# One decode layer, four edits: head 0's softmax on its own, head 6's scores by halves, c and x in SyncE's queue, block-diagonal queries by GpSimd

## The chip, the cores and the metric

The kernel runs on one core of a Trainium2 chip. TensorE (PE) multiplies matrices into PSUM, which has eight banks of 512 float32 per partition; VectorE (DVE), ScalarE (ACT) and GpSimd (POOL) work on tiles of 128 partitions; SyncE (SP) only issues transfers here, and sixteen DMA engines carry them. Each engine runs its instructions in the order in which they were written and waits on semaphores for the others. The metric is device time in microseconds (us), the median of the runs. Times inside an execution count from the first instruction of its profile, its span.

## The reference, cut to what matters

One token (D = 512) goes through attention over a cache of 32768 positions, 32 query heads on 8 key and value heads of 128, and then through a dense layer with ReLU. Both are modulated by a condition vector c.

```python
mod = (_silu(c) @ w_mod).reshape(c.shape[0], 6, 1, -1)
sa, ca, ga, sb, cb, gb = (mod[:, 0].copy(), mod[:, 1].copy(), ...)
h = _layernorm(x, axis=-1) * (1 + ca) + sa
# _A_ref(h): q = h @ wq, 32 heads of 128; each cache head serves 4 of them
scores = jnp.einsum('bhqd,bhkd->bhqk', q, k) * Dh ** (-0.5)
p = _softmax(scores, axis=-1)
o = jnp.einsum('bhqk,bhkd->bhqd', p, v)          # then @ wo
x = x + ga * _A_ref(h, A_k_cache, A_v_cache, A_wq, A_wo)
h = _layernorm(x, axis=-1) * (1 + cb) + sb
x = x + gb * _B_ref(h, B_w1, B_w2)               # relu(h @ w1) @ w2
```

Keys and values are 8 tiles of 8.39 MB each, bfloat16. With the weights that makes 149.4 MB, and every byte is read once.

## The kernel before, in words

**The ring and the stream of loads.** SBUF holds a ring of three slots of 8.39 MB. What is loaded into them, in order, is: w_mod and w_q together (`first`), K0, K1, V0, K2, K3, V1, K4, K5, V2, K6, K7, V3, V4, V5, V6, V7, and then W_o, w1 and w2 (`load_tail`). Each `Tenant` takes the slot of the tenant three before it, so `Tenant.load` (line 228) makes its transfer wait for the last use of that one: K3 waits for the scores of head 1, which read K1, V1 for the product PV(0) with V0, K4 for the scores of head 2, V4 for those of head 6, V5 for those of head 7. In full: slot 0 holds `first`, V0, V1, V2, V3, V6; slot 1 holds K0, K2, K4, K6, V4, V7; slot 2 holds K1, K3, K5, K7, V5 and the tail. All these transfers are issued by SyncE, one after the other; one that waits holds up those behind it. c and x, 1 KB each, are brought into `cx_row` (16 rows of 64) by two transfers from GpSimd's queue (line 285), and the transfers of K0 and K1 wait for both.

**The prologue.** VectorE spreads `cx_row` into a block-diagonal tile (line 327), PE turns it into columns, and the sigmoid, the modulation (24 matmuls with w_mod), a layer norm and the query projection (32 matmuls with w_q) follow. `qrep_sb` (line 456) then holds all queries, repeated per strip of 32 partitions.

**Keys.** A key tile arrives with positions on the partitions. VectorE turns it in place, four transposes (`turn`, line 469) of 128x4096 float32 words, a quarter each. Then `scores` runs 64 matmuls of 512 columns: the weights are `qbd`, where the four queries of the head stand block-diagonally (one block of 32 partitions per strip), shifted from step to step so that all results gather in two banks, one per half G of the tile. A first half needs turns 0 and 1, a second half turns 2 and 3. `build_qbd(g)` (line 463) writes the queries of head g into `qbd` with four ScalarE copies; it waits for the scores of head g - 1, which read the same tile. Only head 7 runs its scores by halves; all others run both halves in one loop after their four turns.

**Softmax.** Heads go in pairs. `maxima` (line 500) reduces a head's two banks; `softmax` turns the maxima on PE (line 510), reduces and spreads them on VectorE (lines 511 and 513), turns them back (line 517), and ScalarE makes the bias and one exponential per head (line 521) into `Pall`. `turn_p` (line 530) transposes both heads' P at once; `sums` and `inverse` (line 544) make the reciprocal of the sum. PV(g) multiplies P of head g with value tile g (64 matmuls). `blocks(g)` (lines 573 and 576) and `o_cols(g)` gather its result in Y and in columns.

**Order.** It is written out by hand. `k_event(h)` gives: the sums of the last pair, four turns, the scores, the queries of the next head, the inverse, and the blocks of an open product; after an odd head, the maximum of the even one before it. `v_event(g)` follows after heads 1, 3 and 5 with g = 0, 1, 2: the odd head's maximum, the softmax of the pair, `turn_p`, and PV(g). So PV(0) stands behind the scores of head 1, PV(1) behind those of head 3, and PV(2) behind those of head 5. After head 7 come PV(3), the last softmax, PV(4) to PV(7) and the output projection, the second layer norm and the dense layer. `keep_clock` inserts idle matmuls there.

Of the kernel before, what the change touches and what calls it, by code (L numbers as in the profile page):

```python
# [9 lines left out]
ALU = mybir.AluOpType  # L10
AX = mybir.AxisListType
# [10 lines left out]
class Flow:  # L22
# [12 lines left out]
    def op(self, eng, run, r=(), w=(), after=(), n=1, dma=False):  # L35
        o = Op(eng, run, n, dma)
        deps = list(after)
        for k in r:
            deps += self.writers.get(k, [])
        for k in w:  # L40
            deps += self.writers.get(k, [])
            deps += self.readers.get(k, [])
        known = self.known[eng]
        for d in deps:
            if d.eng == eng and eng == "pe" and not d.dma:
                continue
            if known.get(d.src, 0) >= d.idx:
                continue
            o.waits.append(d)
        best = {}  # L50
        for d in o.waits:
            if d.src not in best or best[d.src].idx < d.idx:
                best[d.src] = d
        o.waits = []
        for d in sorted(best.values(), key=lambda d: -len(d.clock)):
            if known.get(d.src, 0) >= d.idx:
                continue
            o.waits.append(d)
# [12 lines left out]
        self.ops.append(o)  # L71
        return o
# [5 lines left out]
    def semaphores(self):  # L78
        sems = {e: self.tc.alloc_semaphore(f"of_{e}") for e in self.engine if e != "sp"}
        at = {e: 0 for e in sems}  # L80
        for o in self.ops:
            if o.dma:
                o.sem, o.val = self.tc.alloc_semaphore(f"of_{o.src[0]}{o.src[1]}"), 16
            elif o.used:
                at[o.eng] += o.n
                o.sem, o.val = sems[o.eng], at[o.eng]
# [15 lines left out]
def kernel(  # L102
    ctx, tc, A_x, A_k_cache, A_v_cache, A_wq, A_wo, B_x, B_w1, B_w2, c, w_mod, out,
):
    nc = tc.nc
    P = 128
# [62 lines left out]
    QW = P + 4 * 7  # L169
    qbd = sb("qbd", [P, 4, QW], BF16)  # L170
    mask4 = sb("mask4", [P, REP])
    cmask, rsel_f, rsel = {}, {}, {}
    for n in sorted({n * REP for _, n in WOP}):
        cmask[n] = sb(f"cmask{n}", [P, P // n])
        rsel_f[n] = sb(f"rsel_f{n}", [P, n])
        rsel[n] = sb(f"rsel{n}", [P, n], BF16)
    smask = sb("smask", [16, 4])
    place32 = sb("place32", [P, 32])
# [52 lines left out]
    def rows(src):  # L231
        return src.rearrange("p a b -> p (a b)") if len(src.shape) == 3 else src

    first = Tenant()
    first.load("wm", 0, KT * 6 * D, rows(w_mod.rearrange("(p kt) n -> p kt n", p=P)))
    WQ0 = KT * 6 * D
    first.load("wq", WQ0, KT * Hq * Dh, rows(A_wq.rearrange("(p kt) n -> p kt n", p=P)))
    TMP0 = WQ0 + KT * Hq * Dh
# [41 lines left out]

    wo, w1, w2, spare = [], [], [], []

    for i, src in enumerate((c[0], A_x[0, 0])):
        op(
            "pool", lambda i=i, src=src: nc.gpsimd.dma_start(
                out=cx_row[8 * i:8 * i + 8], in_=src.rearrange("(a n) -> a n", a=8)),
            (), [("cx", i)], dma=True,
        )

    for kind, g in order[:2]:  # L290
        load_tile(kind, g, after=f.writers[("cx", 0)] + f.writers[("cx", 1)])

    def identity(t, key):
        pool(lambda: G_.memset(t, 0.0), (), [key])
# [12 lines left out]
    col_at = col.rearrange("p (kt w) -> p kt w", w=CW)[:, :, 96]  # L307
    first.use(pool(lambda: G_.memset(col, 0.0), (), ["col"]))

    dve(lambda: V.memset(bank(0), 0.0), (), ["b0"])  # L310
    dve(lambda: V.memset(bank(1), 0.0), (), ["b1"])
    dve(lambda: V.memset(bank(2), 0.0), (), ["b2"])
    dve(lambda: V.memset(bank(3), 0.0), (), ["b3"])
    dve(lambda: V.memset(bank(6)[:, 0:REP + KT], 0.0), (), ["b6"])
    oT_ps, attnT_ps = bank(6)[:, 0:REP], bank(6)[:, REP:REP + KT]
    small = bank(7)
# [2 lines left out]
        out=pick8, in0=ident_bf[0:16, 0:8], in1=ident_bf[0:16, 8:16], op=ALU.add), ["ident_bf"], ["pick8"])  # L319

    def fold(o, src, how, key, **kw):
        dve(lambda: V.tensor_reduce(out=o, in_=src.rearrange(how, **kw), op=ALU.add, axis=AX.X), ["ident_f"], [key])

    fold(cmask[8], ident_f, "p (c r) -> p c r", ("cmask", 8), r=8)
    dve(lambda: V.tensor_copy(out=cx_sel, in_=cmask[8][0:16, 0:2]), [("cmask", 8)], ["cx_sel"])
    cx_bd = tmpB.bitcast(BF16)[0:16, 0:512].rearrange("p (b n) -> p b n", b=8)
    first.use(dve(lambda: V.tensor_tensor(  # L327
        out=cx_bd, in0=cx_row.unsqueeze(1).to_broadcast([16, 8, D // 8]),
        in1=pick8.unsqueeze(2).to_broadcast([16, 8, D // 8]), op=ALU.mult,
    ), [("cx", 0), ("cx", 1), "pick8"], ["tmpB"]))  # L330

    def xc_mm(inc):
        for kt in range(KT):
# [11 lines left out]

    fold(mask4, ident_f, "p (x q) -> p q x", "mask4", q=REP)
    for n in cmask:
        if n != 8:
            fold(cmask[n], ident_f, "p (c r) -> p c r", ("cmask", n), r=n)
        fold(rsel_f[n], ident_f, "p (c r) -> p r c", ("rsel_f", n), r=n)  # L350
        dve(lambda n=n: V.tensor_copy(out=rsel[n], in_=rsel_f[n]), [("rsel_f", n)], [("rsel", n)])
    fold(smask, ident_f[0:16, 0:16], "p (s q) -> p s q", "smask", q=REP)
    fold(place32, ident_f, "p (j m) -> p m j", "place32", m=32)
    fold(rowpick, ident_f, "p (j m) -> p j m", "rowpick", m=32)
    qsel = mask4[0:16, :]

# [99 lines left out]
    dve(lambda: V.tensor_copy(out=qrep_sb, in_=qrep_ps), ["b5"], ["qrep"])  # L456

    def build_qbd(g):
        d, s = qbd, qrep_sb
        for a in range(4):  # L460
            o = AP(d.tensor, d.offset + 32 * a * d.ap[0][0] + 4 * 7 + 32 * a, [[d.ap[0][0], 32], [QW, 4], [1, 4]])
            i = AP(s.tensor, s.offset + 32 * a * s.ap[0][0] + REP * g, [[s.ap[0][0], 32], [Hq, 4], [1, 4]])
            act(lambda o=o, i=i: S.copy(out=o, in_=i), ["qrep"], ["qbd"])  # L463


    def turn(h, q):
        t = K[h]
        x = t.ap[:, CH * Dh * q:CH * Dh * (q + 1)].bitcast(F32)
        t.use(dve(lambda: V.transpose(out=x, in_=x), [("k", h, q)], [("kt", h, q)]))  # L469
# [56 lines left out]
    def turn_p(hs):  # L526
        n, i, k = len(hs), hs[0] % 2, hs[0] % 4
        keys = [("P", h % 4) for h in hs]
        pf = Pall[:, k:k + n, :].rearrange("p h f -> p (h f)")
        dve(lambda: V.transpose(out=pf, in_=pf), keys, keys)  # L530
# [277 lines left out]
    f.semaphores()  # L808
    with tc.tile_critical():
        f.emit()  # L810
        nc.scalar.wait_ge(sent.sem, 16)

# [28 lines left out]
```

## Time and profile before

The kernel took 365.78 us, median of 3 runs (364.48 to 366.78). The profiled execution took 364.59 us, its span is 362.8 us.

| | busy us | share of the span | instructions |
|---|---|---|---|
| PE matmuls | 281.1 | 77% | 1283 |
| PE weight loads | 115.2 | 32% | 1283 |
| VectorE | 195.5 | 54% | 187 |
| ScalarE | 31.5 | 9% | 69 |
| GpSimd | 4.2 | 1% | 17 |
| SyncE's DMA queue | | 96% of 16 engines | 4760 packets, 149.43 MB |

The mean rate is 412 GB/s over the span, and TensorE's mean granted clock 0.924. Where times to landing are given, they count from the issue of a transfer to the moment when its waiters may go on. In stretches of a microsecond the DMA share scatters and can come out above 1; that it is 0 means that nothing moved. "L160" is the line of the matmul helper, so matmuls are told apart by what they read: `ring,qbd` are scores, `ring,Pall` are products with V.

### The profile page before, as it was taken

What the parts mean: (1) busy time and instruction counts of PE and PEld (TensorE: products, weight loads), DVE (VectorE), ACT (ScalarE), POOL (GpSimd) and SP (SyncE); (2) the same over time, 40 slices, a digit from 0 to 9 for tenths busy, and PEclk for the clock granted to TensorE, in tenths of its full rate; (3) what the DMA queues carried; (4) which work ended last, traced back from release to release, by engine and by line L of the source; (5) the groups of instructions that cost most, each with busy time, mean ns of one, the idle gap of its engine ahead of it and who ended that gap; (6) DMA issues with size and microseconds to landing.
All of it is one profiled execution on the core that took longest, in us unless ns stands there. A gap on an engine that the chain in (4) does not pass through costs nothing.

```text
span 362.8 us, 4525 instructions
## 1 busy us (share of the span) xinstructions
PE 281.1 (77%) x1283; PEld 115.2 (32%) x1283; DVE 195.5 (54%) x187; ACT 31.5 (9%) x69; POOL 4.2 (1%) x17
## 2 busy tenths in 40 slices
PE   0659005969199978889496979598999999799996
PEld 0223002424034423323142423133343334334434
DVE  4430797960399992169998039999220500321142
ACT  1020300000700000040000050000000400000000
POOL 4000000000000000000000000000000000000000
PEclk9987655999869998999699999989999999999999
DMA  8998999899988989998999899989998999999970
GB/s 317 431 502 369 462 455 441 376 462 462 426 383 347 457 369 448 455 462 369 448 455 449 376 455 455 441 376 462 455 434 385 455 405 448 419 425 430 414 302 2
DMA packets 4831, 149.52 MB, mean 412 GB/s; under 512 B 600, under 2 KB 856, under 8 KB 1752
## 3 DMA queue, kind: packets, MB, share of 16 engines
q1 hardware_dynamic: 4760, 149.43, 96.0%
q8 instruction: 4, 0.07, 0.1%
q14 instruction: 3, 0.02, 0.0%
q0 software_dynamic: 64, 0.00, 0.0%
HBM read 149.42 MB, written 0.00 MB: 412 GB/s over the span
## 4 chain that ended last, share of the span: by engine, by line
PE 49%; DVE 24%; DMA 23%; ACT 2%; issue 1%; POOL 0%; SPq 0%; POOLq 0%
PE banks L160 48%; DMA ring<-in_A_k_cache_dram 21%; DVE ring L469 19%; DMA cx_row<-in_A_x_dram 2%; DVE Pall L530 1%; ACT Pall L521 1%; DVE Y L576 1%; DVE m_p L500 1%; ACT L521 0%; DVE Y L573 0%; DVE Mrow L511 0%; ACT qbd L463 0%; PE banks L510 0%; DVE ring L619 0%; PE banks L517 0%
## 5 line engine op out<-in xcount | busy, mean ns | idle before, releaser
L160 PE MATMUL banks<-ring,qbd 128*128 x512 | 122.4, 395 | 40.8 <-DVE ring L469 29.9
L469 DVE STREAM_TRANSPOSE ring<-ring 128x4096 f32<-128x4096 f32 x32 | 139.3, 4410 | 4.3 <-DMA ring<-in_A_k_cache_dram 4.3
L160 PE MATMUL banks<-ring,Pall 128*16 x512 | 120.7, 386 | 10.1 <-DVE Lexp L531 6.5
L160 PEld LDWEIGHTS banks<-ring,qbd 128*128 x512 | 50.6, 99 | 109.8 <-issue 59.8
L160 PEld LDWEIGHTS banks<-ring,Pall 128*16 x512 | 45.2, 89 | 81.7 <-issue 38.1
L500 DVE TENSOR_REDUCE m_p<-banks 128x1 f32<-128x1024 f32 x8 | 9.6, 1203 | 53.1 <-PE banks L160 53.1
L463 ACT COPY qbd<-qrep_sb 32x16 bf16<-32x16 bf16 x32 | 6.4, 201 | 187.8 <-PE banks L160 186.3
L160 PE MATMUL banks<-ring 128*128 x56 | 17.1, 480 | 3.9 <-DVE ring L437 2.4
L530 DVE STREAM_TRANSPOSE Pall<-Pall 128x2048 bf16<-128x2048 bf16 x4 | 9.2, 2312 | 10.0 <-ACT Pall L521 10.0
L590 DVE TENSOR_TENSOR oT_sb<-banks,Linv 128x4 bf16<-128x4 f32 x8 | 1.2, 153 | 20.7 <-PE banks L160 20.7
L160 PEld LDWEIGHTS banks<-ring 128*128 x56 | 6.6, 118 | 13.5 <-issue 9.7
L600 DVE CAST o<-banks 128x4 bf16<-128x4 f32 (+2 forms) x4 | 0.7, 166 | 18.0 <-PE banks L160 18.0
L160 PE MATMUL banks<-cx_sel,ring 16*128 16x2 bf16 x4 | 0.3, 171 | 11.2 <-DVE ring L327 11.2
L521 ACT ACTIVATE Pall<-banks,nbias 128x1024 bf16<-128x1024 f32 x8 | 8.8, 1109 | 0.1
L576 DVE SCALAR_TENSOR_TENSOR Y<-banks,smask,Y 16x128 f32<-16x128 f32 x24 | 8.1, 339 | 0.8
L511 DVE TENSOR_REDUCE Mrow<-banks 2x4 f32<-2x128 f32 x4 | 1.1, 279 | 13.8 <-PE banks L510 13.8
L573 DVE TENSOR_SCALAR Y<-banks,smask 16x128 f32<-16x128 f32 x8 | 2.5, 314 | 9.9 <-PE banks L160 9.9
L476 ACT COPY banks<-zero_t 128x2048 f32<-128x2048 f32 x4 | 7.5, 1868 | 0.1
L421 ACT ACTIVATE std_ln<-negvar_ln,eps_t 128x1 f32<-128x1 f32 x2 | 0.6, 295 | 64.8 <-DVE negvar_ln L418 64.8
L444 DVE STREAM_TRANSPOSE ring<-banks 128x512 f32<-128x512 f32 x2 | 1.3, 695 | 8.9 <-PE banks L160 8.9
L160 PE MATMUL banks<-qbd,ident_bf 128*128 128x512 bf16 x19 | 5.6, 381 | 0.0
L160 PE MATMUL banks<-mask,Y 16*128 16x4 f32 x16 | 3.0, 258 | 1.8 <-DVE Y L576 1.8
(112 smaller groups left out, 69.1 us busy)
## 6 DMA issues: line engine op xcount, KB each, us to landing
ring<-in_A_v_cache_dram SPq DMA_DIRECT2D x3, 4096.0 KB, 25.6
ring<-in_A_wq_dram SPq DMA_DIRECT2D x1, 4096.0 KB, 19.6
ring<-in_A_v_cache_dram SPq DMA_DIRECT2D x2, 2048.0 KB, 32.4
ring<-in_w_mod_dram SPq DMA_DIRECT2D x1, 3072.0 KB, 10.4
ring<-in_A_wo_dram SPq DMA_DIRECT2D x1, 2048.0 KB, 25.8
ring<-in_B_w_dram SPq DMA_DIRECT2D x1, 1344.0 KB, 32.3
ring<-in_A_wo_dram SPq DMA_DIRECT2D x1, 1024.0 KB, 27.9
ring<-in_A_wo_dram SPq DMA_DIRECT2D x2, 512.0 KB, 29.1
```

The lines of the kernel that those rows point to most:

```text
L160: return T.matmul(o, lhsT=lhsT, rhs=rhs, start=start, stop=stop, skip_group_check=True)
L444: first.use(dve(lambda i=i: V.transpose(out=q_cols[:, i, :], in_=bank(2 + i)), [f"b{2 + i}"], ["tmpB" if i == 0 else "col"]))
L463: act(lambda o=o, i=i: S.copy(out=o, in_=i), ["qrep"], ["qbd"])
L469: t.use(dve(lambda: V.transpose(out=x, in_=x), [("k", h, q)], [("kt", h, q)]))
L476: act(lambda: S.copy(out=banks[:, b:b + n, :].rearrange("p g f -> p (g f)"), in_=zero_t.to_broadcast([P, 512 * n]),), ["zero"], [f"b{b + i ...
L500: dve(lambda: V.reduce_max(out=m_p[:, i:i + 1], in_=banks[:, b:b + 2, :].rearrange("p g f -> p (g f)"), axis=AX.X), [f"b{b}", f"b{b + 1}"] ...
L511: dve(lambda: V.tensor_reduce(out=Mrow[0:n], in_=small[0:n, 0:P].rearrange("o (x q) -> o q x", q=4), op=ALU.max, axis=AX.X), ["b7"], ["Mrow"])
L521: act(lambda h=h, b=b, j=j: S.activation(out=Pall[:, h % 4, :], in_=banks[:, b:b + 2, :].rearrange("p g f -> p (g f)"), func=ACT.Exp, bias ...
L530: dve(lambda: V.transpose(out=pf, in_=pf), keys, keys)
L573: dve(lambda: V.tensor_scalar(out=Y, in0=o[:, 0], scalar1=smask[:, 3:4], scalar2=None, op0=ALU.mult), [f"b{b}", "smask"], ["Y"])
L576: dve(lambda s=s: V.scalar_tensor_tensor(out=Y, in0=o[:, s], scalar=smask[:, 3 - s:4 - s], in1=Y, op0=ALU.mult, op1=ALU.add), [f"b{b}", "Y ...
L590: dve(lambda: V.tensor_tensor(out=o_g, in0=oT_ps, in1=Linv[:, g % 4, :], op=ALU.mult), ["b6", ("Linv", g % 4)], [("oT", g)])
```

## The change

Four edits and some smaller ones.

- c and x are loaded by five transfers in SyncE's queue, behind w_mod and ahead of w_q: c as 8 rows of 64, x as 4, 2, 1 and 1 rows. K0 and K1 no longer wait for them.
- Head 0's maximum and softmax are written between the third and fourth turn of K1, its `turn_p` after the fourth, both ahead of the scores of head 1. After those, only head 1's softmax and `turn_p` are left ahead of PV(0).
- Head 6's scores run by halves, as head 7's do: the first after turns 0 and 1, four matmuls a loop step, the second after turns 2 and 3, eight a step.
- `build_qbd` becomes one GpSimd product of the queries with a 0/1 tile `strip`, 64 elements per partition, over all 128 partitions.
- The smaller ones: one memset for four banks, the 0/1 tiles reduced straight to bfloat16 by a maximum instead of a sum and a copy, one tile (`strip`) more, and transfers that share semaphores where one is known to be over before the next is issued.

```diff
     def semaphores(self):
+        lanes = []
         for o in self.ops:
             if o.dma:
-                o.sem, o.val = self.tc.alloc_semaphore(f"of_{o.src[0]}{o.src[1]}"), 16
+                free = [x for x in lanes if o.clock.get(x[1].src, 0) >= x[1].idx]
...
+                free[0][2] += 16
+                o.sem, o.val = free[0][0], free[0][2]
...
     first.load("wm", 0, KT * 6 * D, rows(w_mod.rearrange("(p kt) n -> p kt n", p=P)))
+    cx_of = [(c[0], 0, 8), (A_x[0, 0], 8, 4), (A_x[0, 0], 12, 2), (A_x[0, 0], 14, 1), (A_x[0, 0], 15, 1)]
+    for i, (src, r, n) in enumerate(cx_of):
+        at = 64 * (r % 8)
+        op(
+            "sp", lambda src=src, r=r, n=n, at=at: nc.sync.dma_start(
+                out=cx_row[r:r + n], in_=src[at:at + 64 * n].rearrange("(a n) -> a n", a=n)),
+            (), [("cx", i)], dma=True,
+        )
...
-    for i, src in enumerate((c[0], A_x[0, 0])):
-        op(
-            "pool", lambda i=i, src=src: nc.gpsimd.dma_start(
-                out=cx_row[8 * i:8 * i + 8], in_=src.rearrange("(a n) -> a n", a=8)),
-            (), [("cx", i)], dma=True,
-        )
-
     for kind, g in order[:2]:
-        load_tile(kind, g, after=f.writers[("cx", 0)] + f.writers[("cx", 1)])
+        load_tile(kind, g)
...
-    dve(lambda: V.memset(bank(0), 0.0), (), ["b0"])
...
+    dve(lambda: V.memset(banks[:, 0:4, :], 0.0), (), [f"b{i}" for i in range(4)])
...
-    fold(cmask[8], ident_f, "p (c r) -> p c r", ("cmask", 8), r=8)
-    dve(lambda: V.tensor_copy(out=cx_sel, in_=cmask[8][0:16, 0:2]), [("cmask", 8)], ["cx_sel"])
+    fold(cx_sel, ident_f[0:16, 0:16], "p (c r) -> p c r", "cx_sel", r=8)
...
+    fold(strip, ident_f, "p (a c) -> p a c", "strip", a=4)
...
     def build_qbd(g):
-        d, s = qbd, qrep_sb
-        for a in range(4):
...
-            act(lambda o=o, i=i: S.copy(out=o, in_=i), ["qrep"], ["qbd"])
+        o = AP(qbd.tensor, qbd.offset + 4 * 7, [[qbd.ap[0][0], P], [QW, 4], [32, 4], [1, 4]])
+        pool(lambda: G_.tensor_tensor(
+            out=o, in0=qrep_sb[:, :, REP * g:REP * (g + 1)].unsqueeze(2).to_broadcast([P, 4, 4, REP]),
+            in1=strip.unsqueeze(1).unsqueeze(3).to_broadcast([P, 4, 4, REP]), op=ALU.mult,
+        ), ["qrep", "strip"], ["qbd"])
...
         for u in range(4):
+            if h == 1 and u == 3:
+                maxima(0)
+                softmax((0,))
             turn(h, u)
-            if h == LAST and u % 2:
+            if h >= LAST - 1 and u % 2:
                 scores(h, (u // 2,), 1 + u // 2)
-        if h < LAST:
+        if h == 1:
+            turn_p((0,))
+        if h < LAST - 1:
             scores(h, (0, 1), 1)
...
-        if h % 2:
+        if h % 2 and h > 1:
             maxima(h - 1)
...
         maxima(hs[-1])
-        softmax(hs)
+        now = hs if g else hs[1:]
+        softmax(now)
         finish()
-        turn_p(hs)
+        turn_p(now)
```

More of the change, by code (lines that the diff above doesn't have):

```diff
@@ L80, in semaphores @@
         at = {e: 0 for e in sems}
+        lanes = []
         for o in self.ops:
             if o.dma:
-                o.sem, o.val = self.tc.alloc_semaphore(f"of_{o.src[0]}{o.src[1]}"), 16
+                free = [x for x in lanes if o.clock.get(x[1].src, 0) >= x[1].idx]
+                if not free:
+                    lanes.append([self.tc.alloc_semaphore(f"of_dma{len(lanes)}"), None, 0])
+                    free = lanes[-1:]
+                free[0][1] = o
+                free[0][2] += 16
+                o.sem, o.val = free[0][0], free[0][2]
             elif o.used:
@@ L171 @@
     mask4 = sb("mask4", [P, REP])
-    cmask, rsel_f, rsel = {}, {}, {}
+    cmask, rsel = {}, {}
     for n in sorted({n * REP for _, n in WOP}):
         cmask[n] = sb(f"cmask{n}", [P, P // n])
-        rsel_f[n] = sb(f"rsel_f{n}", [P, n])
         rsel[n] = sb(f"rsel{n}", [P, n], BF16)
     smask = sb("smask", [16, 4])
-    place32 = sb("place32", [P, 32])
+    place32, strip = sb("place32", [P, 32]), sb("strip", [P, 4])
     rowpick = sb("rowpick", [P, KT])
@@ L308 @@
     first.use(pool(lambda: G_.memset(col, 0.0), (), ["col"]))
-    dve(lambda: V.memset(bank(0), 0.0), (), ["b0"])
-    dve(lambda: V.memset(bank(1), 0.0), (), ["b1"])
-    dve(lambda: V.memset(bank(2), 0.0), (), ["b2"])
-    dve(lambda: V.memset(bank(3), 0.0), (), ["b3"])
+    dve(lambda: V.memset(banks[:, 0:4, :], 0.0), (), [f"b{i}" for i in range(4)])
     dve(lambda: V.memset(bank(6)[:, 0:REP + KT], 0.0), (), ["b6"])
@@ L321, in fold @@
     def fold(o, src, how, key, **kw):
-        dve(lambda: V.tensor_reduce(out=o, in_=src.rearrange(how, **kw), op=ALU.add, axis=AX.X), ["ident_f"], [key])
-    fold(cmask[8], ident_f, "p (c r) -> p c r", ("cmask", 8), r=8)
-    dve(lambda: V.tensor_copy(out=cx_sel, in_=cmask[8][0:16, 0:2]), [("cmask", 8)], ["cx_sel"])
+        dve(lambda: V.tensor_reduce(out=o, in_=src.rearrange(how, **kw), op=ALU.max, axis=AX.X), ["ident_f"], [key])
+    fold(cx_sel, ident_f[0:16, 0:16], "p (c r) -> p c r", "cx_sel", r=8)
     cx_bd = tmpB.bitcast(BF16)[0:16, 0:512].rearrange("p (b n) -> p b n", b=8)
@@ L329 @@
         in1=pick8.unsqueeze(2).to_broadcast([16, 8, D // 8]), op=ALU.mult,
-    ), [("cx", 0), ("cx", 1), "pick8"], ["tmpB"]))
+    ), [*[("cx", i) for i in range(len(cx_of))], "pick8"], ["tmpB"]))
     def xc_mm(inc):
@@ L347 @@
     for n in cmask:
[L348 to L351, printed above, removed]
+        fold(cmask[n], ident_f, "p (c r) -> p c r", ("cmask", n), r=n)
+        fold(rsel[n], ident_f, "p (c r) -> p r c", ("rsel", n), r=n)
     fold(smask, ident_f[0:16, 0:16], "p (s q) -> p s q", "smask", q=REP)
     fold(place32, ident_f, "p (j m) -> p m j", "place32", m=32)
+    fold(strip, ident_f, "p (a c) -> p a c", "strip", a=4)
     fold(rowpick, ident_f, "p (j m) -> p j m", "rowpick", m=32)
@@ L458, in build_qbd @@
     def build_qbd(g):
-        d, s = qbd, qrep_sb
-        for a in range(4):
-            o = AP(d.tensor, d.offset + 32 * a * d.ap[0][0] + 4 * 7 + 32 * a, [[d.ap[0][0], 32], [QW, 4], [1, 4]])
-            i = AP(s.tensor, s.offset + 32 * a * s.ap[0][0] + REP * g, [[s.ap[0][0], 32], [Hq, 4], [1, 4]])
-            act(lambda o=o, i=i: S.copy(out=o, in_=i), ["qrep"], ["qbd"])
+        o = AP(qbd.tensor, qbd.offset + 4 * 7, [[qbd.ap[0][0], P], [QW, 4], [32, 4], [1, 4]])
[3 more added lines that the diff above has]
+        ), ["qrep", "strip"], ["qbd"])
     def turn(h, q):
@@ L810 @@
         f.emit()
-        nc.scalar.wait_ge(sent.sem, 16)
+        nc.scalar.wait_ge(sent.sem, sent.val)
 _INS = ['A_x', 'A_k_cache', 'A_v_cache', 'A_wq', 'A_wo', 'B_x', 'B_w1', 'B_w2', 'c', 'w_mod']
```

## The prediction

> **What bounds the kernel now.** I read the profile page's slices first. The DMA row, busy tenths of the sixteen engines, is at 8 or 9 from end to end:
>
> ```profile
> DMA  8998999899988989998999899989998999999970
> ```
>
> So I listed every large load with its issue time and time to landing. From w_q to V5 each landing comes 19.3 to 19.7 us after the one before (8.39 MB in 19.35 us, 434 GB/s), in the order of issue, with one exception: V1 lands 22.9 us after K3. V1's issue in SyncE's timeline (start, length):
>
> ```profile
> 117.53 0.33 SPq L228 DMA_DIRECT2D ring<-in_A_v_cache_dram  x1
> ```
>
> its time to landing in the list of issues:
>
> ```profile
> ring<-in_A_v_cache_dram SPq DMA_DIRECT2D x1, 23.1
> ```
>
> and three of the microseconds around it (length, busy time of PE, PEld, DVE, ACT and POOL, granted clock, DMA share, GB/s):
>
> ```profile
> 115.00:116.00 1.00, 1.00 (x6) 0.42 (x5) 1.00 (x1) 0.00 (x0) 0.00 (x0) 1.00 0.00 0
> 116.00:117.00 1.00, 1.00 (x6) 0.45 (x5) 1.00 (x1) 0.00 (x0) 0.00 (x0) 1.00 0.01 0
> ...
> 118.00:119.00 1.00, 1.00 (x5) 0.53 (x6) 0.93 (x4) 0.00 (x0) 0.00 (x0) 1.00 2.75 918
> ```
>
> The queue is empty for 3.5 us, because V1 takes V0's slot and waits for PV(0) to end. Issued into an empty queue a tile lands 23.1 us later; to continue the stream it must be issued 23.1 - 19.35 = 3.75 us before its predecessor lands. The other tiles make that with 0.9 to 3.6 us to spare.
>
> Next the chain that ended last, where compute walks beside the stream:
>
> ```profile
> 59.74 17.43 DVE ring L469 x4
> 77.18 0.35 issue
> 77.53 14.11 PE banks L160 x64
> ...
> 91.66 1.24 DVE m_p L500
> ...
> 94.28 1.28 ACT L521
> ...
> 97.91 2.31 DVE Pall L530
> ...
> 100.58 17.25 PE banks L160 x66
> ...
> 119.39 17.34 DVE ring L469 x4
> ...
> 236.30 15.76 PE banks L160 x64
> ```
>
> These are K1's four turns, scores(1), the softmax of both heads, PV(0), K3's turns, and scores(6). From 236.3 to 346 PE is the chain almost without a break, so a microsecond saved there counts until a load is late. V5 lands at 269.5 + 26.2 = 295.7 and PV(5) starts at 299.81: 4.1 us of room, the smallest; V4 has 9, V6 and V7 7 to 11, W_o, w1 and w2 6 to 7.
>
> Third, the stretches where PE resumes after idling:
>
> ```profile
> 74.20:77.50 3.30, 0.03 (x1) 0.00 (x0) 3.30 (x2) 0.81 (x4) 0.00 (x0) 1.00 0.83 357
> 100.60:106.60 6.00, 6.00 (x15) 1.96 (x16) 6.00 (x2) 0.00 (x0) 0.00 (x0) 0.50 0.86 371
> 236.30:239.70 3.40, 3.40 (x9) 1.22 (x10) 3.27 (x4) 0.00 (x0) 0.00 (x0) 0.50 0.76 328
> ```
>
> After 3.3 us of idling before scores(1) the granted clock stays at 1.00. After 8.9 us before PV(0) it is 0.50 for 6.0 us, after 4.5 us before scores(6) for 3.4 us. With scores(0) (4.0), scores(3) (3.6) and scores(4) (3.8) that makes five cold starts of 4.2 us on average, each losing half: 1.7 to 3.0 us, mean 2.1.
>
> **Part by part.**
>
> *Softmax of head 0 inside K1's turns.* Three turns end at 59.74 + 3 x 4.36 = 72.8. VectorE then waits for scores(0), which end at 74.2; maximum, PE transpose, Mrow and copy take 2.15 (91.64 to 93.79 in the same chain), so the fourth turn, queued behind them, runs from 76.4 to 80.8, and scores(1) start at 81.1, **3.6 us later** than 77.53. PE has then idled 6.9 us. The trace has no such stretch here; the cold loss lies between 0 (3.3 us kept the clock) and 3.0 (8.9 us), and 6.9 lies among the rows that lost it: I take 2.1. scores(1) end at 81.1 + 14.1 + 2.1 = 97.3 =: S, not 91.64.
>
> In return PV(0) needs only P of head 0, which is ready. It starts behind head 1's two PE transposes, at S + 2.5 (scores(3) to PV(1): 152.84 to 155.37), instead of 8.9 later, and at full clock, as PV(1) did. At 14.0 to 14.7 (PV(4), PV(3), same loop) it ends near 114.2, not 117.4. V1's hole closes.
>
> But K3 waits for scores(1): issued at 97.3, when it had to go at 98.4 - 3.75 = 94.7, it finds the queue empty and lands at 97.3 + 23.1 = 120.4 (now 117.8). **The hole moves from V1 to K3**; V1 lands at 139.75 (now 140.6).
>
> VectorE: one exponential and half a transposition (1.16) end head 1's softmax; the 1.28 us table load is hidden beside K1's fourth turn. K2's turns start at S + 5.1 = 102.4 (now 100.2), K3's at 121.3, after the 1.5 us of Y. scores(2) start at 120.15 after PE idled 5.5 us: cold, 2.1. With 14.0 (scores(4) less its cold loss) to 15.3 (the row itself) they end at 136.3 to 137.6; K4 had to go at 139.75 - 3.75 = 136.0, a hole of 0.3 to 1.6, say 0.9. K4 lands at 160.0, as now. scores(3) follow without the idling that cost 1.8, and end at 153.2 (now 152.84). K5 lands at 179.35, as now, so up to K6's turns **nothing is won or lost**.
>
> The Trainium skill, "TensorE: Matmul & The Clock Gate", Part 1, states that about 3.4 us of idling in a free-running window halves the clock, and that a busy window of that length restores it. That speaks against this part: by it both new gaps must be cold, for 3.4 to 6.8 us each; as an estimate from that page the loss would be 1.7 to 3.4 and the sum some 0.9 us worse. The five rows agree.
>
> *Head 6's scores by halves.* scores(6, first half) need two turns, done at 227.2, and PE, free after PV(2) and the sums at 231.8: no wait of 4.5 us, no cold start. A half with a four-matmul loop takes 8.85 (scores(7), 253.45 to 262.3), the other 7.1: both end at 247.75 instead of 252.06.
>
> *Queries by GpSimd.* Between scores(6) and scores(7) PE waits 1.39 us for four ScalarE copies. One GpSimd product of 64 elements has no row; 128x128 memsets and selects took 0.20 to 0.29, 128x1 ones 0.10. From 0.1 to 4.4 (should it wait out a VectorE turn), I take 0.3, beside the 0.38 of the Y product: 0.5. scores(7) then run 248.25 to 264.2 (K7's halves are turned at 246.1 and 254.8), now 269.4: **5.2 us ahead**. The other seven builds lie beside turns. PV(3) and PV(4) follow (14.7, 1.2, 14.0, and 0.55): ready at 294.7, but V5 lands at 295.75. PV(5) starts at 295.85 instead of 299.81, **-3.95 us**; 1.2 of the 5.2 goes to the wait. The later loads keep 1.8 us or more.
>
> *c and x in SyncE's queue.* Five issues of about 0.45 delay w_q's issue from 1.40 to 3.6 and go ahead of K0 and K1, all behind 3.1 MB of w_mod: no hole. They land behind w_mod (0.95 + 10.4 = 11.35): between 10.37 (now) and 21.0 (w_q), I take 11.6, nearest to the transfer ahead of it. The prologue moves 1.2 us: qrep is ready at 39.6, K0 lands at 40.37, nothing lost. K0's and K1's wait for c and x hid nothing, since w_q lands at 21.0.
>
> *The rest* (one memset for four, folds straight to bf16, one fold more, shared semaphores): VectorE idles from 5.9 to 10.5 and 15.2 to 20.7: nothing.
>
> **Sum.** The profiled execution took 364.59, 1.8 around its span of 362.8. 364.59 - 3.95 = 360.6. It is 1.2 below the median of 365.78; its cold starts at scores(3) and scores(6), which go, were the shortest, so part of that 1.2 is what goes: I add 0.8. **361.4 us.**
>
> **Rivals.**
> *The clock holds* at scores(1) and (2): S = 95.2, K3's hole 0.5, K4's none; V5 lands at 292.75, PE is ready at 292.55: 358.4. For: 3.3 us kept it. Against: 3.5 and 4.5 did not.
> *GpSimd waits for VectorE.* At 4.30 a VectorE cast of 16x2 took 1.59 us beside GpSimd's memsets (128x4 casts take 0.17), so the two can hold each other up. If the build for head 7 waits out a turn (mean 2.2, at most 4.4), PE is ready at 296.9 to 299.1: 362.5 to 364.7; if all of K7's turns, until 254.8, 367.1. Against: a reduction at 3.98 ran in its usual 0.29 beside the same memsets.
> The Trainium skill, "SBUF — State Buffer", "Who interferes with whom", blocks only VectorE's two-port modes and two-input instructions; by that turns would not hold the build, which no row shows.
> *c and x come with w_q* (slower). At 21.0 qrep is ready at 49.0 instead of 38.4, 8.7 us after K0's landing. K2 must go at 75.3, but goes at 82.9: a hole of 7.6, and S, 8.7 later, widens K3's from 2.6 to 3.7. V5 lands 8.7 after the forecast's: 370.1. It costs from a landing of 12.3 on, microsecond for microsecond, and turns the sign at 16.7. Against: loads landed in order of issue.
> *The change does nothing in head 0 and 1*: that is in the forecast.
>
> **Chances.** Forecast 0.54 (its own spread 359.8 to 363.5), clock holds 0.15, GpSimd waits 0.17, late c and x 0.08, others 0.06. One per cent, 3.7 us, is about what a measurement can tell: faster (under 362.1) 0.36 of the forecast and 0.15 of the clock, 0.51; slower 0.10; same 0.39. The range of 358.3 to 365.3 spans both bounds of the two cold losses (0 to 3.0 each: 358.4 to 363.2), a turn's wait for GpSimd (364.7) and c landing within a microsecond past its room.
>
> **What would show it.** K3's landing near 120 and V1's near 140 with no idle queue between; the low clock at 81 and 120 and none at 100, 139 and 232; scores(7) done near 264; PV(5) starting with V5's landing. Wrong if K3 lands by 118.5, if scores(7) end after 267, or if c lands after 12.3.

## The result and the profile after

The changed kernel takes 362.9 us, median of 18 runs (360.43 to 365.81), against 365.87 for the kernel before on the same chip (18 runs, 363.95 to 369.6): a ratio of 0.9918, 95% interval 0.9888 to 0.9947. That is 3.0 us less, 1.5 above the forecast of 361.4 and inside its range. The profiled execution took 365.78 us (span 364.0) and is one of the two slowest of the 18, so its last microseconds are not those of the median; a second profile of the same kernel, from the experiments, took 363.49 (span 361.7) and stands beside it below. Where a run is named in what follows, "after" is the first, "repeated" the second.

The DMA row of the page of after, busy tenths in 40 slices, now has a dent in the eleventh slice (91 to 100 us):

```profile
DMA  8998999899699899999999999999899989999980
```

SyncE's timeline of after (start, length) tells which load that is:

```profile
75.58 24.21 SPq L234 DMA_DIRECT2D ring<-in_A_k_cache_dram  x2
117.60 0.33 SPq L234 DMA_DIRECT2D ring<-in_A_v_cache_dram  x1
```

The first line holds K2 (75.58) and K3, whose issue ends the row at 99.79. V1 follows at 117.60. The microseconds around both follow (length; busy time of PE, PEld, DVE, ACT, POOL; granted clock, DMA share, GB/s). In these rows a packet is counted whole in the microsecond in which it starts, and one of 64 KB took 2.42 us in the stream; so a share of 0 says that no packet started, and not that nothing moved:

```profile
97.00:98.00 1.00, 1.00 (x6) 0.46 (x5) 0.00 (x0) 0.00 (x0) 0.00 (x0) 1.00 0.15 66
98.00:99.00 1.00, 1.00 (x6) 0.40 (x5) 0.00 (x0) 0.00 (x0) 0.00 (x0) 1.00 0.01 0
99.00:100.00 1.00, 0.38 (x2) 0.00 (x0) 0.58 (x1) 0.00 (x0) 0.29 (x1) 1.00 0.00 0
...
116.00:117.00 1.00, 1.00 (x7) 0.39 (x5) 1.00 (x1) 0.00 (x0) 0.00 (x0) 1.00 0.15 66
117.00:118.00 1.00, 0.89 (x5) 0.36 (x3) 1.00 (x2) 0.00 (x0) 0.00 (x0) 1.00 0.46 197
```

The packets themselves, from the transfers' records in the trace, say which dip is a hole. The sixteen engines finish K2 one by one between 97.37 and 99.78, and the first packets of K3 start at 100.42: between 0.6 and 3.1 us in which an engine had nothing to move, and ahead of V1 before it was much the same (K3 finished between 116.12 and 117.30, V1's first packets at 118.49; the 3.5 us of the prediction are what its landing lost, not a time in which nothing moved). Ahead of V1 in after there is no hole: the engines finish K3 between 120.36 and 120.85 and start on V1 at 120.37 to 120.87. Why K3 is late stands in the chain that ended last (start, length, engine and buffer):

```profile
58.48 17.02 PE banks L167 x64
75.53 1.24 DVE m_p L502
...
77.65 4.37 DVE ring L471
...
82.36 17.03 PE banks L167 x64
...
102.05 1.21 ACT Pall L523 x2
...
104.57 17.33 DVE ring L471 x4
...
123.33 17.34 DVE ring L471 x4
```

The fourth turn of K1 stands behind the maximum of head 0, scores(1) start at 82.36 and end at 99.38. After that one exponential is left, and the chain goes on with VectorE, from K2's turns to K3's without a break. The clock in stretches of after, in the columns of the windows above:

```profile
78.10:88.40 10.30, 6.04 (x15) 2.18 (x16) 5.56 (x4) 2.51 (x4) 0.00 (x0) 0.50 0.93 394
...
102.00:105.40 3.40, 3.40 (x9) 1.18 (x9) 2.12 (x3) 3.09 (x4) 0.00 (x0) 0.50 0.71 308
122.50:125.90 3.40, 3.40 (x9) 1.12 (x8) 3.33 (x4) 0.00 (x0) 0.00 (x0) 0.50 1.34 578
139.00:155.00 16.00, 13.95 (x64) 6.13 (x64) 3.25 (x3) 0.00 (x0) 0.00 (x0) 1.00 1.05 455
231.00:249.00 18.00, 17.54 (x74) 6.97 (x74) 17.54 (x10) 0.00 (x0) 0.00 (x0) 1.00 0.98 422
300.00:303.40 3.40, 3.40 (x10) 1.12 (x9) 0.00 (x0) 0.00 (x0) 0.00 (x0) 0.50 0.97 414
```

The clock is low for scores(1) and scores(2), as forecast, and full for scores(3) and scores(6), as forecast; it is also low at the start of PV(0) and of PV(5), which was not. The end, from TensorE's timeline of the kernel before (start, length, and in brackets the idle time ahead), scores(6) and PV(5):

```profile
236.30 15.74 PE L160 MATMUL banks<-ring,qbd 128*128 x64 [4.55 <-DVE Y L573]
...
299.81 13.98 PE L160 MATMUL banks<-ring,Pall 128*16 x64
```

and from that of after:

```profile
233.23 15.89 PE L167 MATMUL banks<-ring,qbd 128*128 x64
249.05 0.38 PE L167 MATMUL banks<-mask,Y 16*128 16x4 f32 x2
249.96 16.08 PE L167 MATMUL banks<-ring,qbd 128*128 x64 [0.53 <-POOL qbd L462]
...
295.42 0.39 PE L167 MATMUL banks<-Lexp,ones_f 128*128 128x8 f32 x2
299.51 15.66 PE L167 MATMUL banks<-ring,Pall 128*16 x64 [3.71 <-DMA ring<-in_A_v_cache_dram]
```

scores(6) start right behind the sums (232.99), without the 4.55 us of waiting and the cold start of before; scores(7) are done at 266.04 instead of 269.46. TensorE is ready for PV(5) at 295.8, where it was at 299.8 before, and then **waits 3.71 us for V5**. In this execution the wait and the cold start behind it (15.66 us for PV(5) instead of 13.98) give back all of it: PV(5) ends at 315.17, where it ended at 313.79 before. The repeated profile has the same place with a shorter wait:

```profile
297.18 3.18 PE L167 MATMUL banks<-ring,Pall 128*16 x14 [0.31 <-DMA ring<-in_A_v_cache_dram]
```

There TensorE itself is ready only at 296.9, and V5 lands just behind that. In both, V5 is complete later than in the kernel before. When each tile was complete (last packet of the last of the sixteen engines, from the transfers' records in the traces; a waiter goes on 0.4 to 0.9 later; the last column is an experiment, head 1's halves):

| complete, us | before | after | repeated | head 1's halves |
|---|---|---|---|---|
| V0 | 78.59 | 78.85 | 78.61 | 78.88 |
| K2 | 97.95 | 99.78 | 97.96 | 99.75 |
| K3 | 117.30 | 120.85 | 118.64 | 119.33 |
| V1 | 140.19 | 141.53 | 139.26 | 138.68 |
| K6 | 217.58 | 219.82 | 217.63 | 216.20 |
| V3 | 256.27 | 258.48 | 256.58 | 254.84 |
| V4 | 275.62 | 279.28 | 277.00 | 274.16 |
| V5 | 295.31 | 298.62 | 296.34 | 293.47 |

An unbroken stream would need 11 x 19.35 = 212.85 us from V0 to V5. Before lost 3.9 us over that, after 6.9, the repeated run 4.9.

The column of the kernel before is an early one. By the same records V5 was complete at 295.75, 296.22, 297.22, 298.26, 298.33 and 298.80 in the six profiles of experiments that leave head 0's softmax where it was, and at 296.44 and 296.64 in two more that move it as the change does. So the kernel before's profile, with 295.31, has the earliest V5 of these and of the two profiles of the changed kernel, and a later V5 is not shown to be the work of head 0's part.

### The profile page after: what moved, and what is told of

It is laid out like the page before. It is cut to its first block, busy times and chain, and to the rows that moved or that the text cites. A ratio compares the mean times of both kernels' runs of the same rounds, so it can differ in the third digit from the quotient of the medians.

```text
span 364.0 us, 4521 instructions
## 1 busy us (share of the span) xinstructions
PE 282.3 (78%) x1285; PEld 115.9 (32%) x1285; DVE 193.8 (53%) x186; ACT 25.3 (7%) x38; POOL 5.4 (1%) x23
## 4 chain that ended last, share of the span: by engine, by line
PE 46%; DVE 30%; DMA 19%; issue 2%; ACT 1%; SPq 1%; POOL 0%
PE banks L167 45%; DVE ring L471 25%; DMA ring<-in_A_k_cache_dram 10%; DMA ring<-in_A_v_cache_dram 9%; DVE m_p L502 1%; DVE Y L578 1%; DVE Pall L532 1%; ACT Pall L523 1%; SPq L246 0%; DVE Mrow L513 0%; PE banks L512 0%; DVE Y L575 0%; DVE Pall L515 0%; SPq L234 0%; DVE ring L621 0%
## 5 line engine op out<-in xcount | busy, mean ns | idle before, releaser
L167 PE MATMUL banks<-ring,qbd 128*128 x512 | 125.0, 400 | 41.2 <-DVE ring L471 30.7
L167 PE MATMUL banks<-ring 128*128 x56 | 15.4, 444 | 3.8 <-DVE ring L439 2.4
L520 ACT ACTIVATE nbias<-banks 128x2 f32<-128x2 f32 (+1 forms) x5 | 0.9, 172 | 227.4 <-PE banks L519 227.4
L532 DVE STREAM_TRANSPOSE Pall<-Pall 128x2048 bf16<-128x2048 bf16 (+1 forms) x5 | 9.4, 1874 | 7.7 <-ACT Pall L523 7.7
L513 DVE TENSOR_REDUCE Mrow<-banks 2x4 f32<-2x128 f32 (+1 forms) x5 | 1.4, 278 | 13.5 <-PE banks L512 13.5
L462 POOL TENSOR_TENSOR qbd<-qrep_sb,strip 128x64 bf16<-128x64 bf16 x8 | 2.3, 292 | 243.0 <-PE banks L167 209.3
```

The lines of the kernel that those rows point to most:

```text
L167: return T.matmul(o, lhsT=lhsT, rhs=rhs, start=start, stop=stop, skip_group_check=True)
L462: pool(lambda: G_.tensor_tensor(out=o, in0=qrep_sb[:, :, REP * g:REP * (g + 1)].unsqueeze(2).to_broadcast([P, 4, 4, REP]), in1=strip.unsqu ...
L513: dve(lambda: V.tensor_reduce(out=Mrow[0:n], in_=small[0:n, 0:P].rearrange("o (x q) -> o q x", q=4), op=ALU.max, axis=AX.X), ["b7"], ["Mrow"])
```

## The experiments

**Which part makes the gain.** Each part was put alone into the kernel before, and head 0's part was taken out of the changed kernel.

*Head 0's softmax alone:*

```diff
         for u in range(4):
+            if h == 1 and u == 3:
+                maxima(0)
+                softmax((0,))
             turn(h, u)
...
+        if h == 1:
+            turn_p((0,))
...
```

> The kernel before with head 0's softmax moved alone. My theory: K3's hole of 2.5 to 5 us in place of V1's, scores(1) cold, compute up to K6 within 1 us of before, no gain at the end: 365.5 to 367.5. Rival (it shortens the chain ahead of PV(0) and that gain arrives): 362 to 363.5.

Measured: 367.03 us (12 runs), ratio 1.0019, interval 0.9993 to 1.0045: nothing won, as expected. Its SyncE timeline shows V1's early issue, its windows the dip ahead of K3:

```profile
73.99 23.46 SPq L228 DMA_DIRECT2D ring<-in_A_k_cache_dram  x2
113.58 0.33 SPq L228 DMA_DIRECT2D ring<-in_A_v_cache_dram  x1
```

```profile
96.00:97.00 1.00, 1.00 (x5) 0.29 (x3) 0.00 (x0) 0.00 (x0) 0.00 (x0) 1.00 0.00 0
97.00:98.00 1.00, 0.05 (x1) 0.00 (x0) 0.91 (x1) 0.81 (x4) 0.00 (x0) 1.00 0.01 0
```

V1 goes 3.95 us earlier than in the kernel before (117.53). K3 is issued at 97.1, when the first engines have just finished K2 (from 96.94 on, the last at 98.22), and its first packets start at 98.1. K3 is complete 21.6 us after K2 and V1 19.6 after K3, where it was 19.35 and 22.9 before: this part alone moves the hole, a little under the 2.5 to 5 us that were expected for it.

*Head 6's scores by halves alone,* in two runs of their own, on the same chip as their kernel before:

```diff
-            if h == LAST and u % 2:
+            if h >= LAST - 1 and u % 2:
                 scores(h, (u // 2,), 1 + u // 2)
-        if h < LAST:
+        if h < LAST - 1:
             scores(h, (0, 1), 1)
```

> The kernel before with head 6's scores by halves alone. My theory: scores(6) start with PV(2)'s end, at full clock, end 4.3 us earlier (5 where the cold start was longer than the profile's 3.4 us); PV(5) then waits little or not for V5, which leaves room for 4.1: 361.6 to 362.6. Rival (the loads at the end are what the kernel waits for): 365 to 366.

Measured: 361.28 us (6 runs, 360.66 to 365.5), ratio 0.9872, interval 0.9836 to 0.9909; 0.3 us below what was expected.

> The kernel before with head 6's scores by halves alone, again, beside the next run on the same chip. Theory (the earlier 361.3 was of six runs that scattered by 5 us, the part is worth the 3 us of the whole change): 361.5 to 363.0. Rival (it is truly better than the whole change): 360.5 to 361.5.

Measured: 363.53 us (7 runs, 361.27 to 363.95), ratio 0.9911, interval 0.9875 to 0.9947; half a microsecond above what was expected. Together the 13 runs have their median at 363.3. In TensorE's timeline of the second, the scores stand behind the sums without a wait:

```profile
233.83 16.00 PE L160 MATMUL banks<-ring,qbd 128*128 x64
251.23 16.16 PE L160 MATMUL banks<-ring,qbd 128*128 x64 [1.09 <-ACT qbd L463]
```

16.00 us against 15.74 before looks like a loss, but this loop runs all at full clock (a half with a four-matmul step is slower by itself), and it starts 2.5 us sooner. As far as these runs can tell, this part alone is worth what the whole change is.

*GpSimd's product alone:*

```diff
-            act(lambda o=o, i=i: S.copy(out=o, in_=i), ["qrep"], ["qbd"])
...
+        pool(lambda: G_.tensor_tensor(
+            out=o, in0=qrep_sb[:, :, REP * g:REP * (g + 1)].unsqueeze(2).to_broadcast([P, 4, 4, REP]),
+            in1=strip.unsqueeze(1).unsqueeze(3).to_broadcast([P, 4, 4, REP]), op=ALU.mult,
+        ), ["qrep", "strip"], ["qbd"])
```

> The kernel before with the block-diagonal queries by GpSimd alone. My theory: only the build for head 7 lies on the path, 1.39 us between scores(6) and scores(7) become 0.5: 0.9 less, 364.7 to 365.3. Rival (GpSimd waits out VectorE's turns): 366 or more, with the product longer than 0.29 us or started late.

Measured: 365.89 us (12 runs), ratio 0.9985, interval 0.995 to 1.002; this lies between what was expected (364.7 to 365.3) and the rival (366 or more). In microseconds the interval is 1.8 faster to 0.7 slower: the small gain that was expected lies inside it, and so does none. The trace shows the step itself, in TensorE's timeline:

```profile
255.44 4.85 PE L160 MATMUL banks<-ring,qbd 128*128 x17 [0.53 <-POOL qbd L461]
```

The wait is 0.53 us where four copies made it 1.09.

*c and x in SyncE's queue alone:*

```diff
+    cx_of = [(c[0], 0, 8), (A_x[0, 0], 8, 4), (A_x[0, 0], 12, 2), (A_x[0, 0], 14, 1), (A_x[0, 0], 15, 1)]
+    for i, (src, r, n) in enumerate(cx_of):
...
-        load_tile(kind, g, after=f.writers[("cx", 0)] + f.writers[("cx", 1)])
+        load_tile(kind, g)
...
```

> The kernel before with c and x in SyncE's queue alone. My theory: c and x land near 11.4, the prologue ends about 1 us later, all hidden behind K0's landing: 365.5 to 366.3, no difference. Rival (the prologue reaches the turns of K0): over 367; rival (the loads of K0 and K1 gain from not waiting): under 364.5.

Measured: 366.23 us (12 runs), ratio 0.9998, interval 0.9968 to 1.0028: no difference, as expected.

*The changed kernel without head 0's part,* twice:

```diff
-            if h == 1 and u == 3:
-                maxima(0)
-                softmax((0,))
             turn(h, u)
...
-        now = hs if g else hs[1:]
+        now = hs
```

> The changed kernel with both heads' softmax together again, behind the scores of head 1; everything else as changed. My theory (head 0's part only moves the queue's hole from V1 to K3): V1's hole is back (3 to 3.5 us), K3's is gone, scores(1) start near 77.5 at full clock; V5 lands as in the kernel before, PV(5) waits for it: 361.8 to 363.0, that is the changed kernel's 362.9 or up to 1 us less. Rival (head 0's softmax is what wins): 365 to 366.

Measured: 364.84 us (12 runs, 361.89 to 366.85), ratio 0.9947, interval 0.9913 to 0.9981. That is neither what the theory nor what the rival said, and 3.6 us above the halves alone on the same chip, though it differs from them only by GpSimd's product and c and x, which alone cost nothing, and by the smaller edits, which were not run alone. The holes are where the theory had them, ahead of V1 (complete 23.1 us after K3) and not ahead of K3 (19.3 after K2), but scores(1) are cold (15.77 us), and TensorE waits 3.84 us for V5. So both were run again, side by side (the halves' repetition is told above).

> The changed kernel without head 0's separate softmax, again: head 6's halves, GpSimd's product, c and x in SyncE's queue. Theory (its 364.8 and the 361.3 of the halves alone differ by the phase of the clock and by the lag of single DMA engines, not by GpSimd or c and x): 362.0 to 364.0, and within 1.5 us of the run before. Rival (GpSimd's product, or c and x ahead of w_q, costs 2 us or more once the halves are there): 364.0 to 366.0, 2 us or more above the run before.

Measured: 362.77 us (6 runs, 360.87 to 364.37), ratio 0.9895, interval 0.9854 to 0.9936; 0.8 us below the halves alone this time. The order turned round: the earlier difference did not come again, and no cost of GpSimd's product or of c and x beside the halves is seen. All 18 runs of this kernel have their median at 364.2, the 30 of the changed kernel (with those below) at 363.0. Head 0's part, in the changed kernel, thus makes 1.2 us between two medians of runs that scatter by 5; that it makes anything is not shown.

*The changed kernel again:*

> The changed kernel itself, for a second profile and as the measure beside the others: 362.9 +- 0.6. My theory: K3's hole of 2.5 to 5 us, no hole at V1, PV(5) starts with V5's landing; where the cold starts of scores(0) and scores(1) fall shorter than in its first profile (6.0 us each), the hole and the span are shorter by about half of the difference.

Measured: 363.47 us (12 runs), ratio 0.9918, interval 0.9881 to 0.9956, the same as the first time. Its scores(1) and PV(0), in TensorE's timeline:

```profile
80.59 16.35 PE L167 MATMUL banks<-ring,qbd 128*128 x64 [4.48 <-DVE ring L471]
99.47 13.98 PE L167 MATMUL banks<-ring,Pall 128*16 x64
```

**Is it V5 that sets the end?** V5 was loaded in two halves, each with its own half of PV(5), so that TensorE waits for 4.2 MB instead of 8.4:

```diff
-    pieces = {("v", LAST - 1): [(0, 2), (2, 4)], ...}
+    pieces = {("v", 5): [(0, 2), (2, 4)], ("v", LAST - 1): [(0, 2), (2, 4)], ...}
...
-    pv(5, (0, 1, 2, 3), 2)
+    pv(5, (0, 1), 4)
+    pv(5, (2, 3), 4)
```

> The changed kernel with V5 loaded in two halves and PV(5) run in two halves, so that its first half waits for the first half of V5 alone. Theory (the end of the changed kernel is set by the landing of V5): PV(5) starts 0.3 to 3.8 us earlier (the waits seen so far) and without the cold start of 1.7 us behind the longest of these waits; time 1 to 3 us below the changed kernel's 362.9, so 360.0 to 362.0. Rival (the loads behind V5 take the gain back, or the end is set by PE alone): 362.5 to 363.5.

Measured: 360.46 us (6 runs, 359.29 to 362.36), ratio 0.984, interval 0.9799 to 0.9881, as the theory had it. Its PV(5):

```profile
294.14 0.39 PE L167 MATMUL banks<-Lexp,ones_f 128*128 128x8 f32 x2
294.45 13.98 PE L167 MATMUL banks<-ring,Pall 128*16 x64
```

No wait, no low clock, 13.98 us instead of 15.66, although the second half of V5 is complete only at 296.66, 2.2 us after PV(5) has begun. No computation ahead of PV(5) was touched, and the median is 2.4 us below the changed kernel's 362.9; the interval of its ratio lies wholly below the changed kernel's (0.9888 to 0.9947). So the wait for the whole of V5 does set the end of the changed kernel, by about that much in the median; in the two profiles of the changed kernel it was 3.71 and 0.31 us. The loads behind V5 did not take the gain back.

**Is it the cold start of scores(1) that makes K3 late?** 18 idle matmuls were put ahead of scores(1), into a bank that nobody reads, to keep the clock:

```diff
                 maxima(0)
                 softmax((0,))
+                warm(18)
...
```

> The changed kernel with 18 idle matmuls of 512 columns in PE's gap between head 0's two maximum transposes and scores(1), into a bank that is free there. If the cold start costs what I say (half of 3.4 to 6.8 us), scores(1) run at full clock and end 1.7 to 3.4 us earlier, K3's hole shrinks by as much and V5 lands that much earlier: 360.0 to 361.5. Rival (the clock at scores(1) does not matter, since the hole or the end is set elsewhere): 362.5 to 363.5.

Measured: 363.03 us (12 runs; 360.57 to 366.82, and one of 406.39 at a mean granted clock of 0.738, whose cause is not known), ratio 0.9904, interval 0.9863 to 0.9944. The rival's number came, though the clock did stay up:

```profile
77.27 5.75 PE L167 MATMUL banks<-qbd,ident_bf 128*128 128x512 bf16 x18
82.86 14.09 PE L167 MATMUL banks<-ring,qbd 128*128 x64
```

At full clock scores(1) end at 96.95. That is still 2.2 us later than the 94.7 at which K3 had to be issued by the forecast's reckoning, so the hole stays. It is no earlier than the cold 96.94 of the repeated run for two reasons: scores(0) ended 1.2 us later in this one (74.92 against 73.69), and the idle matmuls, which end at 83.02, outlast K1's fourth turn (81.42) and hold scores(1) up by another microsecond. So this edit gave back about half of the 2.3 us that it won in scores(1), and it tests the cold start less sharply than it was meant to. Taking the low clock away in this way did not move the median.

**Can both holes be closed?** What moves the hole is that the fourth turn of K1, and all of scores(1) with it, waits for head 0's maximum. Here scores(1) run by halves: the first half behind turns 0 and 1, head 0's softmax behind the fourth turn:

```diff
+            turn(h, u)
             if h == 1 and u == 3:
                 maxima(0)
                 softmax((0,))
-            turn(h, u)
-            if h >= LAST - 1 and u % 2:
+            if (h == 1 or h >= LAST - 1) and u % 2:
                 scores(h, (u // 2,), 1 + u // 2)
...
-        if h < LAST - 1:
+        if h < LAST - 1 and h != 1:
             scores(h, (0, 1), 1)
```

> The changed kernel with head 1's scores by halves too: the first half after turns 0 and 1, head 0's maximum and softmax behind K1's fourth turn, between the two halves on PE. Then no turn waits for scores(0), PE has no gap ahead of scores(1), and K3 is issued near 91.5 with V1 near 108: no hole at either, V1 to V5 land 3 to 3.5 us earlier than before, PV(5) starts at V5's landing near 292.5. My theory (the two holes and the cold start are what the changed kernel still pays): 357.3 to 359.5. Rival (something else holds the end, the transfers or PE): 361.5 to 363.

Measured: 360.42 us (6 runs, 358.93 to 362.13), ratio 0.9851, interval 0.9816 to 0.9886; 2.5 us below the changed kernel, though a microsecond above what was expected. TensorE's timeline and SyncE's:

```profile
76.29 8.76 PE L167 MATMUL banks<-ring,qbd 128*128 x32 [0.84 <-POOL qbd L462]
...
86.09 7.16 PE L167 MATMUL banks<-ring,qbd 128*128 x32
95.77 14.42 PE L167 MATMUL banks<-ring,Pall 128*16 x64
```

```profile
75.53 18.13 SPq L234 DMA_DIRECT2D ring<-in_A_k_cache_dram  x2
110.23 0.33 SPq L234 DMA_DIRECT2D ring<-in_A_v_cache_dram  x1
```

scores(1) wait 0.84 us instead of 4.44 and run at full clock (granted 1.00 in the windows over both halves), K3 goes at 93.3 and V1 at 110.23, and in the table above neither leaves a hole (19.58 and 19.35 between K2, K3 and V1). What is left is a hole of 1.5 us ahead of K2, which went at 75.53 when the cold scores(0) let go of its slot: 20.87 us lie between V0 and K2. Without it V5, complete at 293.47, could be so at 292; that this is the microsecond missing was not tested.

**Both remedies at once,** head 1's halves and V5's:

> The kernel with head 1's scores by halves, and V5 and PV(5) by halves as well. Its PV(5) waited 0.68 us for V5. Theory (V5's landing is the bound there too, but only just): 0 to 1 us below its 360.4, so 359.4 to 360.4. Rival (what bounded it is the clock and PE's own work, which the halves lengthen by a second loop): 360.4 to 361.4.

Measured: 359.5 us (6 runs, 357.82 to 361.75), ratio 0.9814, interval 0.9772 to 0.9857, as the theory had it, though the interval overlaps with that of head 1's halves alone. This has the lowest median here, 6.5 us below the kernel before and 3.4 below the changed one. The two remedies, 2.4 and 2.5 alone, don't add up; both shorten the same wait for V5, which was 0.68 us with head 1's halves alone.

## Why the prediction was right, and where it was off

**Part 1, head 0's softmax: right.** "The hole moves from V1 to K3" and "nothing is won or lost" are what the runs showed: alone the part gives 1.0019 (0.9993 to 1.0045), and inside the change its removal makes no difference that the scatter lets through (364.2 against 363.0). The forecast's points against the two profiles:

| | forecast | after | repeated |
|---|---|---|---|
| scores(1) start | 81.1 | 82.36 | 80.59 |
| cold loss in scores(1) (length less 14.1) | 2.1 | 2.9 | 2.25 |
| end of scores(1), S | 97.3 | 99.38 | 96.94 |
| end of PV(0) | 114.2 | 117.57 | 113.45 |
| scores(2) start | 120.15 | 122.27 | 119.83 |
| scores(7) done | 264.2 | 266.04 | 267.0 |
| PV(5) start | 295.85 | 299.51 | 297.18 |

Up to scores(2) the repeated run stays within 0.75 us of every step; at scores(7) it stands right at the 267 that the forecast named as its bound. After is 2 us late from scores(1) on: scores(0) had a cold start of 6.0 us, K1's fourth turn waited 1.3 us longer for it, and scores(1) lost 2.9 us, the bound of 3.0. The rival in which the clock holds is out: both new gaps were cold in both profiles. On this the Trainium skill, "TensorE: Matmul & The Clock Gate", Part 1, which halves the clock after some 3.4 us of idling, agrees with the trace: 2.9 and 1.7 us lost in after. On gaps shorter than that the runs went both ways (last section), and there the runs decide.

**Part 2, head 6's halves: right, but for its start.** No wait and no cold start, and a loop of 15.89 us (forecast 15.95). It started at 233.23 and 234.20 instead of 231.8: in after because S was late, in the repeated run because scores(3) and scores(5) were cold (15.77 and 15.61 us instead of 14.10), which the forecast had denied or not considered.

**Part 3, GpSimd: price right, saving too large.** The product, in GpSimd's timeline, and the turns of K7 that ran beside it, in VectorE's:

```profile
249.20 0.29 POOL L462 TENSOR_TENSOR qbd<-qrep_sb,strip 128x64 bf16<-128x64 bf16 x1 [35.78 <-PE banks L167]
```

```profile
243.89 13.05 DVE L471 STREAM_TRANSPOSE ring<-ring 128x4096 f32<-128x4096 f32 x3
```

0.29 us against the 0.3 taken, and three turns in the 13.05 us that they took before. The rival in which GpSimd waits out a turn is out. But the gap between scores(6) and scores(7) is 0.84 us (249.12 to 249.96), not 0.5, since TensorE needs another 0.46 after the product until its first matmul, which the chain lists as issue: 0.55 was saved of 1.39, where 0.89 was forecast.

**Part 4, c and x: right.** Their first use in after, in VectorE's timeline:

```profile
11.50 0.68 DVE L330 TENSOR_TENSOR ring<-cx_row,pick 16x512 bf16<-16x512 bf16 x1 [8.14 <-DMA cx_row<-in_A_x_dram]
```

They landed by 11.5 (forecast 11.6), far from the 16.7 that would have turned the sign, and alone the part measures 0.9998.

**The step that was off is the stream's, the time at which V5 lands, and with it the 1.2 us that the sum gave to the wait for V5.** "V5 lands at 295.75" took V5 to land as in the kernel before, of which one profile was at hand; all later ones without head 1's halves have V5 later. It counted two holes, 2.6 us ahead of K3 and 0.9 ahead of K4. In after, K3 lost 1.7 and K4 nothing, but four tiles lost time that was not forecast: K2 1.6 (its issue waited for the cold scores(0)), V1 1.3, K6 0.5 and V4 1.45 (with V2's 0.4 that makes the 6.9 of after). The repeated run has K3 1.3, V1 1.3, K6 0.8 and V4 1.1. The price of an empty queue was not one number either: from issue to completion V1 took 22.7 us before and K3 22.7 with head 0's part alone, as the forecast had it, but K3 took 21.4 in after and 21.6 in the repeated run; K3 and V1 together lost 3.0 and 2.6, near what was forecast for K3. So V5 was complete 1.0 to 3.3 us after its time in the kernel before, where the forecast had it as before, and PV(5) started 1.3 to 3.7 later than forecast. In the repeated run TensorE was late by itself as well, ready for PV(5) at 296.9 instead of 294.7 (295.8 in after). Of the 5.2 us ahead, the forecast gave 1.2 to the wait for V5; taking that wait away brought 2.4. By the medians that is 1.2 of the 1.5 us between 361.4 and 362.9; six runs that scatter by 3 us don't give it more exactly.

Two of these, V1's and V4's, are not an empty queue but a slow engine: the engines went on without a pause (V1 was issued 3.3 us before K3 was complete in after, 5.2 in the repeated run). In after the first engine finishes V4 19.34 us after V3, as in an unbroken stream, and the last 20.80; in the repeated run it is 19.33 and 20.42 for V4, and 19.34 and 20.62 for V1. What held the slowest engines up was not tested and stays open.

The chances were less good than the sum. The likeliest call was a gain of more than one per cent (0.51, against 0.39 for less); it came out at 0.8%. That the sum missed by only 1.5 us is in part luck: the holes that it had too large (K3, K4) made up for some of the losses that it did not have (K2, V1, K6, V4, and the low clock at PV(0), PV(5), scores(3) and scores(5)).

## What to carry to other kernels

Where a ring of loads and a chain of compute run side by side, closing a hole by bringing its consumer forward is worth nothing if what is put ahead delays the consumer of the slot before: list for every load the latest issue time that keeps the queue full, and check the neighbours of the one that is mended. A microsecond saved on the compute side counts only up to the next landing; there, loading the tile in pieces is a cheap way to use it (2.4 us here for three lines). With a scatter of 5 us between runs, a part worth 1 us should not be judged by one set of six to twelve runs: the same two kernels changed places between two sets. And a landing time read off one profile has a scatter too: V5's differed by 3.5 us between profiles, more than the whole gain.

## What the runs showed of the hardware that was not expected

The stretches of low clock come in steps of one length, and fall on different matmuls in different executions. In after they are 3.4 us (from 102.0, 122.5 and 300.0) and 10.3 us long (from 78.1), which is three times 3.4. In the repeated run scores(3) and scores(5) took 15.77 and 15.61 us, in after 14.10 each; PV(0) was cold in after (15.66) and warm in the repeated run (13.98). TensorE had idled 2.71 us ahead of the warm scores(3) and 2.92 ahead of the cold one. So a gap of under 3 us is cold in one execution and not in the next, and S alone differs by 2.4 us between the two profiles.

The sixteen DMA engines drift apart. In after the first and the last engine finish K3 0.5 us apart, V1 1.7, K6 2.3, V4 3.8 and V5 3.7; K2, ahead of the empty queue, 2.4. In after, from V1 on, the distance never shrank by more than 0.03 us from one tile to the next, and a tile's waiters go on with the slowest engine. An empty queue doesn't always set it back: the one ahead of K3 did (2.4 to 0.5), but the one ahead of V1 in the kernel before was followed by a greater distance (1.2 at K3, 1.9 at V1). In the kernel before, V5 had 2.0.
